# Other widths of the token pairs, another schedule for the weight factors, and another order of products in two groups

## The chip, the cores and the metric

The kernel runs on one core of a Trainium2 chip. The metric is device time in microseconds (us) of one execution; three runs of the kernel before give a median of 1737.24 us (1734.43 to 1738.43). The engines are TensorE (PE; its weight loads are listed apart as PEld), VectorE (DVE), ScalarE (ACT), GpSimd (POOL) and SyncE (SP), which issues all of this kernel's DMAs. Each engine takes its instructions in the order in which they were put to it.

## The reference

```python
def reference(q, k, v, moe_w_in, moe_w_out, moe2_w_in, moe2_w_out, moe2_alpha):
    # q, k, v: [8, 8, 576, 64]; attention inside chunks of 64 positions
    s = (q_c @ k_c.T) / sqrt(64);  a = softmax(s)
    x = (a @ v_c)                         # -> [4608 tokens, 512]
    h = x @ moe_w_in                      # 512 -> 2048
    x = (h * sigmoid(1.702 * h)) @ moe_w_out        # 2048 -> 512
    h = x @ moe2_w_in                     # 512 -> 2048
    g = max(h, 0) + alpha * min(h, 0)     # one alpha for each of 2048
    return g @ moe2_w_out                 # [4608, 512]
```

The weights arrive as 64-bit floats, taken as pairs of 32-bit words.

## The kernel before

A 64-bit weight is decoded on the chip: ACT takes the absolute value of the high word (L149), DVE puts a 32-bit float together in four passes (L152 to L167). For the matmuls each operand is split into a rounded part and the rest, and each product is made in three passes (high by high, low by high, high by low).

**First layer.** Nine blocks of 512 tokens, each with 16 slots, one for each 128 of the 2048 hidden features: 144 slots. In a slot `emit_h` (L446) runs 12 matmuls into `psH`, ACT's sigmoid (L460), DVE's product `g` (L462), ACT's rounding `gs` (L117) and the rest on DVE (L120). `emit_y` (L469) runs the 12 matmuls into `psY` of two slots earlier. Between these stand, by a table of half slots (`between`), the parts of the attention for later groups of 128 tokens: their loads (`load_qk`, `load_v`), transposes on DVE (L392), matmuls into `psS` and `psX`, the copies of `psX` on ACT (L417). A group of 128 tokens takes four slots. Where it crosses from one of the 8 batches to the next, its loads are cut in two.

**Preparation for the second layer.** The second layer's matrices are taken in halves and multiplied by a scheme of seven products for eight. Its seven weight factors of a block are made during the first layer in 32 steps, one every 3.25 slots from slot 18 on: `prep_load` reads a raw block of four quarters, `prep_abs` and `prep_decode` decode it, `prep_store_a` stores the three factors that are quarters themselves and lets POOL form four sums, `prep_store_b` stores the four others. Both split their four quarters (L222 on ACT, L223 on POOL) into the one tile `st2`, and write from it to DRAM. A loop at the end of the kernel puts the five parts of a step into slots n + 1, n + 2, n + 3, n + 4 and n + 6; each runs at the end of its slot. DMAs of the first layer wait in SP's order: a store that waits for its factors holds the raw loads and the attention's loads behind it.

**Second layer.** Tokens are taken in five pairs of two halves, of `PAIRS` columns each. A pair has four groups of 512 hidden features; a group has seven H products of 24 matmuls (two feature blocks `jj` of 12), in `H_ORDER`, and seven Y products of 24, in `Y_ORDER`. The H products use two accumulators, `psHa` for products 1, 6, 7 and 4, `psHb` for 2, 5 and 3; `ya` and `yb` likewise for Y. Products accumulate over one another (`start` at 1, 2 and 5 only), with read-outs between by ACT (L689, L663) and DVE (L692). The Y products of a group run between the H products of the next, so the first group's H products and the last group's Y products have no partner. `plan_group` gives each part of the work between H and Y a due time on a counter of products: the differences (L716), the rounding `o` on ACT (L706) and the rest on DVE (L711). DVE applies alpha at L666, and L775 and L777 add the Y results into `yacc`. `wi2t` (a ring of 9 tiles) and `w` (a ring of 4) hold the weights, loaded by SP one product at a time as tiles come free. A finished pair is written by `y_out` (L784) in 32 DMAs, the last one by `y_last`.

Of the kernel before, what the change touches and what calls it, by code (L numbers as in the profile page):

```python
# [9 lines left out]
F32 = mybir.dt.float32  # L10
F32R = mybir.dt.float32r
# [19 lines left out]
PREP_FROM = 18  # L31
PREP_EVERY = 3.25

PAIRS = (480, 480, 448, 448, 448)

H_ORDER = (1, 2, 6, 5, 7, 3, 4)
Y_ORDER = (1, 5, 6, 3, 7, 2, 4)
PLACE = {1: 0, 2: 1, 3: 6, 4: 2, 5: 3, 6: 4, 7: 5}

# [6 lines left out]
def tile_chunk_attention_two_ffn(  # L46
# [18 lines left out]
    P = 128  # L65
# [3 lines left out]
    GPB = NB // P  # L69
# [132 lines left out]
    def prep_store(step, lo, hi, t):  # L202
        kind, j, m = step
        dst = wi2[j][:, lo:hi, m] if kind == "wi" else wo2[j // 2][:, lo:hi, j % 2, m]
        nc.sync.dma_start(
            out=dst.rearrange("p i a f -> p i (a f)"),
            in_=t.bitcast(F32).rearrange("p i a f -> p i (a f)"),
        )
# [8 lines left out]
        except StopIteration as done:  # L217
            pr[step] = done.value[0].rearrange("p (q f) -> p q f", q=4)

    def prep_split(step, src):  # L220
        t = prep_p.tile([P, 4, 2, P], F32R, tag="st2", name="st2")
        nc.scalar.copy(t[:, :, 0], src)  # L222
        nc.gpsimd.tensor_tensor(out=t[:, :, 1], in0=src, in1=t[:, :, 0].bitcast(F32), op=ALU.subtract)  # L223
        return t

    def prep_store_a(step):
        u = pr[step]
        t = prep_split(step, u)
        prep_store(step, 0, 3, t[:, 0:3])
        sums = dec_p.tile([P, 4, P], F32, tag="u", name="sums")  # L230
        a11, a12, a22, a21 = (u[:, q] for q in range(4))
        for o, x, y, op in (
            (0, a21, a22, ALU.add), (1, sums[:, 0], a11, ALU.subtract),
            (2, a11, a21, ALU.subtract), (3, a12, sums[:, 1], ALU.subtract),
        ):
            nc.gpsimd.tensor_tensor(out=sums[:, o], in0=x, in1=y, op=op)
        pr[step] = sums

    def prep_store_b(step):
        t = prep_split(step, pr.pop(step))  # L240
        prep_store(step, 3, 7, t)


    def spans(t0, n):
# [17 lines left out]
    def load_qkv(g, names="qkv"):  # L262

        for nm in names:
            if g < GPB:
                t = {
                    "q": lambda: spare(f"wi{NF - GPB + g}", 0),
                    "k": lambda: spare(f"wi{NF - GPB + g}", 1),
                    "v": lambda: spare(f"wo{NF - 1 - g // 2}", g % 2),
                }[nm]()  # L270
            else:
                t = qkv_p.tile([P, 512], F32, tag=nm, name=nm, bufs=2)
            t = t.rearrange("p (h d) -> p h d", h=H)
            for off, n, b, s in spans(g * P, P):
                nc.sync.dma_start(
                    out=t[off:off + n],
                    in_={"q": q, "k": k, "v": v}[nm][b, :, s:s + n, :].rearrange("h p d -> p h d"),
                )
            qkv[g, nm] = t
# [289 lines left out]

    hs = [(p, gr, i, jj) for p in range(NP) for gr in range(NGR) for i in H_ORDER for jj in range(2)]
    ys = [(p, gr, i) for p in range(NP) for gr in range(NGR) for i in Y_ORDER]
    wi_order, wo_order, wi_q, wo_q = list(hs), list(ys), [], []
    turn = {"wi": 0, "wo": 0}
# [19 lines left out]
    def second_layer():  # L595
# [125 lines left out]
        def plan_group(p, gr, u):  # L721

            n = PAIRS[p]
            last = (p, gr) == (NP - 1, NGR - 1)
            times = (23, 25, 27, 30, 35, 39, 43) if last else (27, 30, 34, 36, 44, 46, 49)
            for i, nm, hi in zip(
                (1, 5, 6, 3, 7, 2, 4), ("g11", "t", "t", "g22", "t3", "g21", "t"), times
            ):
                at(u + hi, op_hi, p, gr, i, nm)
                at(u + hi + 1, op_lo, p, gr, i, nm)  # L730
            eng = nc.vector if last else nc.gpsimd
            t1, t2, t3, t4 = (24, 26, 29, 30) if last else (24, 32, 29, 38)
            at(u + t1, diff, n, "t", "g12", "g11", eng)
            at(u + t2, diff, n, "t", "g22", "t", eng)
            at(u + t3, diff, n, "t3", "g22", "g12", eng)
            at(u + t4, diff, n, "t", "g21", "t", nc.gpsimd)
# [122 lines left out]
    with tc.manual_schedule():  # L859
# [49 lines left out]
        ]  # L909
        for i, step in enumerate(steps):  # L910
            n = PREP_FROM + int(i * PREP_EVERY)
            for lag, fn in enumerate((None, prep_load, prep_abs, prep_decode, prep_store_a, None, prep_store_b)):
                if fn:
                    todo.setdefault(("prep", n + lag), []).append(partial(fn, step))


        between = {}
        for g in range(GPB, NG):
            for at, fn in zip((-4, -1, -1, 2, 5), (att_T, att_S, att_E, att_AT, att_PV)):
                if g > GPB or at > 0:  # L920
                    between.setdefault(8 * (g - GPB) + at, []).append((fn, g))
            if g + 1 < NG:
                between[8 * (g - GPB) + 5].append((load_v, g + 1))
            if g + 2 < NG:
                for part in range(8):
                    between.setdefault(max(0, 8 * (g - GPB) - 1 + part), []).append(
                        (partial(load_qk, part), g + 2)
                    )
# [4 lines left out]
        for n in range(NBLK * NF):  # L933
            blk, f = divmod(n, NF)
            for key in list(dec_t):
                split_w(*key)

            def middle():
                nonlocal dec
                for fn, g in between.get(2 * n, []):  # L940
                    fn(g)
                ahead = decode_w(todo.get(("decode", n + 1), []))
                next(ahead)
                for _ in dec:
                    pass
                dec = ahead

            emit_h(n, middle, nc.gpsimd if ("decode", n) in todo else nc.vector)


            ahead_y = {0: (n - 1,), 1: (), NF - 1: (n - 2, n - 1)}.get(f, (n - 2,))
            for m in ahead_y:
                if m >= 0:
                    emit_y(m)
            for fn, g in between.get(2 * n + 1, []):
                fn(g)
            for key in todo.get(("load", n), []):
                load_w(*key)
            for fn in todo.get(("prep", n), []):
                fn()  # L960
            if n == NBLK * NF - NF + 2:

                first.close()
                sec_p = ctx.enter_context(tc.tile_pool(name="second", bufs=1, reuse_waits="tile"))
                second_homes()
                x_load(0)
                for fn in x_sums(0):
                    fn()
            if n >= NBLK * NF - 12 and n % 2 == 0:
                i = H_ORDER[(n - (NBLK * NF - 12)) // 2] if n < NBLK * NF - 0 else None  # L970
                x_hi(0, i)
                x_lo(0, i)
            if n == NBLK * NF - 3:
                more_homes()
# [35 lines left out]
```

## Time and profile before

| what | us |
|---|---|
| median of three runs | 1737.24 |
| the profiled execution | 1733.37 |
| its span, first to last instruction | 1731.6 |
| PE busy | 1631.3 (94%) |
| weight loads on PE | 1366.9 (79%) |
| DVE busy | 1267.8 (73%) |
| ACT busy | 785.2 (45%) |
| POOL busy | 500.4 (29%) |

The profiled execution is one run under the hardware profiler. "Busy" sums the instructions of an engine; the matmuls are pipelined and weight loads overlap them, so a busy PE may still run below its best pace, which is read from the distance between the starts of equal groups of matmuls. The first layer ends near 997 us and the second begins there. The granted clock is 0.98 as a mean over the span.

### The profile page before, as it was taken

The page shows a single profiled execution, that of the slowest core. Times are in us where ns is not written, and L with a number is a line of the kernel's source. Part 1 is how long each engine was busy: PE and PEld are TensorE (multiplying, and loading weights), DVE is VectorE, ACT ScalarE, POOL GpSimd, SP SyncE. Part 2 cuts the span into 40 slices and gives each one's busy share as a digit, 9 for nine tenths or more (in the row PEclk, how much of TensorE's full clock was granted, in tenths as well). Part 3 has the DMA queues.
Part 4 walks back from the last instruction along what each step waited for, and adds up shares of the span by engine and source line. Part 5 has one row for each costly group of instructions (what it writes and reads, how often), then busy time and mean ns, then how long its engine had stood idle before and what let it go on. Part 6 is the DMA issues. An engine that isn't in the chain of part 4 may idle for free.

```text
span 1731.6 us, 25761 instructions
## 1 busy us (share of the span) xinstructions
PE 1631.3 (94%) x9257; PEld 1366.9 (79%) x9259; DVE 1267.8 (73%) x1858; ACT 785.2 (45%) x1098; POOL 500.4 (29%) x382
## 2 busy tenths in 40 slices
PE   7879998999988999989999989999999999999997
PEld 5667876777767777767788878888888998998996
DVE  7998666686666777757774347887788788788776
ACT  5554434344334443434433344555455455554542
POOL 3664122222212222212222024223422423422320
PEclk9999999999999999999999999999999999999999
DMA  8741334444334344334423067669667877977854
GB/s 229 215 115 36 73 88 110 114 109 111 93 92 107 107 110 115 101 97 118 100 62 125 0 214 249 203 180 293 214 204 194 309 217 193 313 212 192 278 180 121
DMA packets 388591, 268.11 MB, mean 155 GB/s; under 512 B 265840, under 2 KB 328048, under 8 KB 388464
## 3 DMA queue, kind: packets, MB, share of 16 engines
q1 hardware_dynamic: 388464, 266.47, 53.8%
q8 instruction: 73, 1.20, 0.3%
q14 instruction: 54, 0.44, 0.1%
HBM read 218.11 MB, written 48.23 MB: 154 GB/s over the span
## 4 chain that ended last, share of the span: by engine, by line
PE 45%; DVE 19%; DMA 8%; SPq 8%; ACT 7%; issue 4%; POOL 2%; DVEq 0%; ACTq 0%; POOLq 0%
PE psYa L759 10%; PE psHa L647 9%; PE psYb L759 7%; PE psHb L647 6%; SPq L297 6%; PE psH L453 6%; PE psY L476 5%; DMA raw<-in_moe_w_in_dram 3%; DMA raw<-in_moe_w_out_dram 3%; DVE g L462 2%; DVE g L666 2%; DVE at L392 2%; ACT gs L117 2%; DVE gs L120 1%; DVE o L711 1%
## 5 line engine op out<-in xcount | busy, mean ns | idle before, releaser
L453 PE MATMUL psH<-xs,wi 128*128 128x512 f32 x1728 | 442.7, 407 | 33.1 <-DVE g L462 29.5
L453 PEld LDWEIGHTS psH<-xs,wi 128*128 128x128 f32 x1728 | 330.6, 195 | 113.6 <-DVE g L462 37.8
L476 PE MATMUL psY<-gs,wo 128*128 128x512 f32 x1728 | 415.1, 390 | 3.6 <-ACT gs L117 3.6
L476 PEld LDWEIGHTS psY<-gs,wo 128*128 128x128 f32 x1728 | 323.7, 188 | 73.2 <-ACT gs L117 5.5
L117 ACT CAST gs<-g 128x512 fp32r<-128x512 f32 x144 | 89.3, 620 | 351.6 <-DVE g L462 351.6
L759 PE MATMUL psYa<-o,w 128*128 128x448 f32 (+1 forms) x960 | 218.6, 376 | 6.3 <-ACT o L706 3.8
L647 PE MATMUL psHa<-xop,wi2t 128*128 128x448 f32 (+1 forms) x960 | 216.0, 374 | 4.8 <-ACT g L663 4.4
L759 PEld LDWEIGHTS psYa<-o,w 128*128 128x128 f32 x960 | 180.2, 189 | 32.1 <-ACT o L706 5.1
L647 PEld LDWEIGHTS psHa<-xop,wi2t 128*128 128x128 f32 x960 | 181.7, 189 | 26.6 <-ACT g L663 4.8
L462 DVE TENSOR_TENSOR g<-psH,g 128x512 f32<-128x512 f32 x144 | 98.4, 683 | 138.5 <-ACT g L460 137.7
L666 DVE SCALAR_TENSOR_TENSOR g<-neg,minus_alpha,g 128x448 f32<-128x448 f32 (+1 forms) x160 | 182.7, 1182 | 6.8 <-ACT g L663 6.7
L759 PE MATMUL psYb<-o,w 128*128 128x448 f32 (+1 forms) x720 | 161.9, 373 | 0.0
L647 PE MATMUL psHb<-xop,wi2t 128*128 128x448 f32 (+1 forms) x720 | 160.1, 371 | 0.0
L120 DVE TENSOR_TENSOR gs<-g,gs 128x512 fp32r<-128x512 f32 x129 | 93.7, 726 | 88.6 <-ACT gs L117 87.9
L716 POOL TENSOR_TENSOR tsum<-g,tsum 128x896 f32<-128x896 f32 (+1 forms) x39 | 92.6, 2375 | 199.7 <-DVE o L711 196.9
L759 PEld LDWEIGHTS psYb<-o,w 128*128 128x128 f32 x720 | 134.8, 188 | 16.9 <-DVE o L711 0.6
L647 PEld LDWEIGHTS psHb<-xop,wi2t 128*128 128x128 f32 x720 | 135.2, 188 | 15.4
L716 POOL TENSOR_TENSOR tsum<-g,g 128x896 f32<-128x896 f32 (+1 forms) x19 | 41.6, 2188 | 350.9 <-DVE g L666 301.9
L392 DVE STREAM_TRANSPOSE at<-e 32x128 f32<-32x128 f32 x448 | 135.5, 302 | 6.7
L662 ACT ACTIVATE neg<-g 128x896 f32<-128x896 f32 (+1 forms) x60 | 58.5, 975 | 124.1 <-DVE g L692 124.1
L460 ACT ACTIVATE g<-psH 128x512 f32<-128x512 f32 x144 | 85.8, 596 | 50.7 <-PE psH L453 50.3
L711 DVE TENSOR_TENSOR o<-tsum,o 128x896 fp32r<-128x896 f32 (+1 forms) x60 | 66.5, 1109 | 46.1 <-ACT o L706 44.0
(117 smaller groups left out, 1898.8 us busy)
## 6 DMA issues: line engine op xcount, KB each, us to landing
wi2t<-wi SPq DMA_DIRECT2D x280, 256.0 KB, 3.8
w<-wo SPq DMA_DIRECT2D x140, 512.0 KB, 3.6
x<-ysb SPq DMA_DIRECT2D x36, 256.0 KB, 2.5
raw<-in_moe_w_in_dram SPq DMA_DIRECT2D x16, 512.0 KB, 5.4
raw<-in_moe_w_out_dram SPq DMA_DIRECT2D x16, 512.0 KB, 4.3
raw<-in_moe_w_in_dram SPq DMA_DIRECT2D x32, 256.0 KB, 3.9
wi<-st SPq DMA_DIRECT2D x16, 512.0 KB, 2.9
raw<-in_moe_w_out_dram SPq DMA_DIRECT2D x32, 256.0 KB, 3.5
```

What stands on the lines that cost most here:

```text
L117: nc.scalar.copy(hi, src)
L120: eng_lo.tensor_tensor(out=lo, in0=src, in1=hi.bitcast(F32), op=ALU.subtract)
L297: nc.sync.dma_start(out=t[r:r + SQ, h // 2, off // SQ:(off + n) // SQ], in_=src[b, h, s:s + n, y * SQ:(y + 1) * SQ].rearrange("(b t) e -> ...
L392: nc.vector.transpose(t[o * SQ:(o + 1) * SQ, :, i * SQ:(i + 1) * SQ], blocks[i * SQ:(i + 1) * SQ, :, o // 2, o % 2, :],)
L453: nc.tensor.matmul(ps, w[:, a, c], xs[:, b, c], start=(i == 0), stop=(i == 3 * KT - 1))
L460: nc.scalar.activation(out=g, in_=ps, func=AF.Sigmoid, scale=1.702)
L462: nc.vector.tensor_tensor(out=g, in0=ps, in1=g, op=ALU.mult)
L476: nc.tensor.matmul(y_t[j][t], w[:, a, t * P:(t + 1) * P], gs[:, b], start=(f == 0 and a + b == 0), stop=(f == NF - 1 and b == 1),)
L647: nc.tensor.matmul(ps, w[:, c, a], x[b][:, c], start=(k == 0 and i in (1, 2, 5)), stop=(k == 5 and i in (2, 3, 4)), skip_group_check=True,)
L666: nc.vector.scalar_tensor_tensor(out=g, in0=neg, scalar=minus_alpha[:, f:f + 1], in1=g, op0=ALU.mult, op1=ALU.add)
L716: eng.tensor_tensor(out=wide(homes[out], n), in0=wide(homes[x], n), in1=wide(homes[y], n), op=ALU.subtract,)
L759: nc.tensor.matmul(ps[:, d, :n], w[:, jj, d, a], x[b][:, jj], start=(k == 0 and i in (1, 5, 2)), stop=(k == 5 and i in (3, 2, 4)), skip_gr ...
```

## The change

The five pairs are 512, 512, 512, 384 and 384 columns wide in place of 480, 480, 448, 448 and 448; both add up to 2304. The first group of the second layer takes its H products in the order 1, 2, 6, 5, 7, 4, 3 (3 and 4 exchanged), the last group in the order 1, 2, 5, 6, 3, 7, 4, and the due times of the work of the first and of the last two groups are others. In the preparation the factors go through two tiles, `sta` with three factors and `stb` with four; the split for the first store handles three quarters in place of four; the absolute value runs in slot n + 3 right behind `emit_h`, where it stood at the end of slot n + 2; the second store comes in slot n + 5 in place of n + 6. `v` has one buffer in place of two from group 4 on, and its load is issued one slot later.

```diff
-PAIRS = (480, 480, 448, 448, 448)
+PAIRS = (512, 512, 512, 384, 384)
 H_ORDER = (1, 2, 6, 5, 7, 3, 4)
+H_FIRST = (1, 2, 6, 5, 7, 4, 3)
+H_LAST = (1, 2, 5, 6, 3, 7, 4)
...
-    def prep_split(step, src):
-        t = prep_p.tile([P, 4, 2, P], F32R, tag="st2", name="st2")
+    def prep_split(src, n, tag):
+        t = prep_p.tile([P, n, 2, P], F32R, tag=tag, name=tag)
         nc.scalar.copy(t[:, :, 0], src)
         nc.gpsimd.tensor_tensor(out=t[:, :, 1], in0=src, in1=t[:, :, 0].bitcast(F32), op=ALU.subtract)
         return t
 
     def prep_store_a(step):
         u = pr[step]
-        t = prep_split(step, u)
-        prep_store(step, 0, 3, t[:, 0:3])
+        prep_store(step, 0, 3, prep_split(u[:, 0:3], 3, "sta"))
...
     def prep_store_b(step):
-        t = prep_split(step, pr.pop(step))
-        prep_store(step, 3, 7, t)
+        prep_store(step, 3, 7, prep_split(pr.pop(step), 4, "stb"))
...
-                t = qkv_p.tile([P, 512], F32, tag=nm, name=nm, bufs=2)
+                t = qkv_p.tile([P, 512], F32, tag=nm, name=nm, bufs=1 if nm == "v" else 2)
...
+    FIRST_G, LAST_G = (0, 0), (NP - 1, NGR - 1)
+    h_order = {FIRST_G: H_FIRST, LAST_G: H_LAST}
...
-            times = (23, 25, 27, 30, 35, 39, 43) if last else (27, 30, 34, 36, 44, 46, 49)
+            times = {
+                FIRST_G: (27, 31, 36, 37, 44, 46, 49), LAST_G: (23, 22, 26, 28, 34, 38, 42),
+                (NP - 1, NGR - 2): (27, 30, 34, 33, 44, 46, 40),
+            }.get((p, gr), (27, 30, 34, 36, 44, 46, 49))
...
-            t1, t2, t3, t4 = (24, 26, 29, 30) if last else (24, 32, 29, 38)
+            t1, t2, t3, t4 = {FIRST_G: (28, 34, 30, 38), LAST_G: (20, 24, 28, 29)}.get(
+                (p, gr), (24, 32, 29, 38)
+            )
...
-            for lag, fn in enumerate((None, prep_load, prep_abs, prep_decode, prep_store_a, None, prep_store_b)):
-                if fn:
-                    todo.setdefault(("prep", n + lag), []).append(partial(fn, step))
+            for what, lag, fn in (
+                ("prep", 1, prep_load), ("abs", 3, prep_abs), ("prep", 3, prep_decode),
+                ("prep", 4, prep_store_a), ("prep", 5, prep_store_b),
+            ):
+                todo.setdefault((what, n + lag), []).append(partial(fn, step))
...
-                between[8 * (g - GPB) + 5].append((load_v, g + 1))
+                between.setdefault(8 * (g - GPB) + 7, []).append((load_v, g + 1))
...
             emit_h(n, middle, nc.gpsimd if ("decode", n) in todo else nc.vector)
+            for fn in todo.get(("abs", n), []):
+                fn()
```

On ACT, one step of the preparation in the first layer. Before (`u<-raw` is the absolute value, `st<-sums` and `st<-u` the splits for the second and the first store, `g` and `gs` the sigmoid and the rounding of a slot):

```order
L117 CAST gs<-g 128x512
L222 CAST st_5476<-sums 128x4x128
L149 ACTIVATE u<-raw_5434 128x512
L460 ACTIVATE g<-psH 128x512
L117 CAST gs<-g 128x512
L460 ACTIVATE g<-psH 128x512
L117 CAST gs<-g 128x512
L417 COPY x<-psX 128x4x64 x2
L222 CAST st_5608<-u 128x4x128
```

And now, the same place in the program:

```order
L225 CAST stb<-sums 128x4x128
L461 ACT_TABLE_LOAD
L461 ACTIVATE g<-psH 128x512
L120 CAST gs<-g 128x512
L461 ACTIVATE g<-psH 128x512
L120 CAST gs<-g 128x512
L152 ACTIVATE u<-raw_5438 128x512
L461 ACTIVATE g<-psH 128x512
L120 CAST gs<-g 128x512
L418 COPY x<-psX 128x4x64 x2
L225 CAST sta<-u 128x3x128
```

The absolute value has moved behind sigmoid and rounding of a later slot, and the two splits go to tiles of their own, the first of them with three quarters.

On PE, the first group of the second layer and the first Y matmuls, before:

```order
L647 MATMUL psHa<-xop,wi2t 128x480 x12
L647 MATMUL psHb<-xop,wi2t 128x480 x12
L647 MATMUL psHa<-xop,wi2t 128x480 x12
L647 MATMUL psHb<-xop,wi2t 128x480 x12
L647 MATMUL psHa<-xop,wi2t 128x480 x12
L647 MATMUL psHb<-xop,wi2t 128x480 x12
L647 MATMUL psHa<-xop,wi2t 128x480 x24
L647 MATMUL psHb<-xop,wi2t 128x480 x12
L759 MATMUL psYa<-o_9641,w_9625 128x480
```

And now:

```order
L653 MATMUL psHa<-xop,wi2t 128x512 x12
L653 MATMUL psHb<-xop,wi2t 128x512 x12
L653 MATMUL psHa<-xop,wi2t 128x512 x12
L653 MATMUL psHb<-xop,wi2t 128x512 x12
L653 MATMUL psHa<-xop,wi2t 128x512 x24
L653 MATMUL psHb<-xop,wi2t 128x512 x12
L653 MATMUL psHa<-xop,wi2t 128x512 x12
L653 MATMUL psHb<-xop,wi2t 128x512 x12
L770 MATMUL psYa<-o_9639,w_9623 128x512
```

The run of two products on `psHa` stood for product 4 and the next group's product 1; now it stands for products 7 and 4, with product 3 on `psHb` behind it.

On DVE, the last group's work ahead of its own first Y products, before (the four `g` with running numbers are g11, g12, g22 and g21 in that order):

```order
L777 TENSOR_TENSOR yacc<-psYa,yacc 128x2x448
L711 TENSOR_TENSOR o_9642<-tsum,o_9641 128x896
L666 SCALAR_TENSOR_TENSOR g_9634<-neg,minus_alpha,g_9634 128x448 x2
L711 TENSOR_TENSOR o_9644<-g_9633,o_9643 128x896
L716 TENSOR_TENSOR tsum<-g_9634,g_9633 128x896
L777 TENSOR_TENSOR yacc<-psYb,yacc 128x2x448
L711 TENSOR_TENSOR o_9646<-tsum,o_9645 128x896
L716 TENSOR_TENSOR tsum<-g_9635,tsum 128x896
L666 SCALAR_TENSOR_TENSOR g_9636<-neg,minus_alpha,g_9636 128x448 x2
L777 TENSOR_TENSOR yacc<-psYa,yacc 128x448 x2
```

And now:

```order
L672 SCALAR_TENSOR_TENSOR g_9632<-neg,minus_alpha,g_9632 128x384 x2
L698 TENSOR_TENSOR g_9633<-psHa,g_9633 128x768
L722 TENSOR_TENSOR tsum<-g_9632,g_9631 128x768
L788 TENSOR_TENSOR yacc<-psYa,yacc 128x2x384
L717 TENSOR_TENSOR o_9640<-tsum,o_9639 128x768
L672 SCALAR_TENSOR_TENSOR g_9633<-neg,minus_alpha,g_9633 128x384 x2
L717 TENSOR_TENSOR o_9646<-g_9631,o_9645 128x768
L722 TENSOR_TENSOR tsum<-g_9633,tsum 128x768
L788 TENSOR_TENSOR yacc<-psYb,yacc 128x2x384
L672 SCALAR_TENSOR_TENSOR g_9634<-neg,minus_alpha,g_9634 128x384 x2
L788 TENSOR_TENSOR yacc<-psYa,yacc 128x384 x2
```

Between the last two additions into `yacc` stand now the two steps of alpha for g21 alone; an `o` and a difference have moved ahead.

## Rows read from the trace of the kernel before

**Rows 1.** Busy time by stretch: window, us, engines, PE clock, DMA share, GB/s.

```profile
150.00:900.00 750.00, 699.71 (x4523) 559.76 (x4522) 523.14 (x1057) 305.04 (x495) 184.50 (x225) 0.98 0.39 100
1316.00:1700.00 384.00, 380.46 (x1850) 346.37 (x1848) 310.65 (x311) 198.04 (x229) 116.97 (x52) 1.00 0.77 232
```

**Rows 2.** Waits, 150 to 900 us: engine, releaser, total us, times, longest us.

```profile
ACT u L149 <- DMA raw<-in_moe_w_in_dram: 41.5, 13, 6.0
ACT u L149 <- DMA raw<-in_moe_w_out_dram: 41.1, 14, 5.0
...
PE psH L453 <- DVE g L462: 18.6, 8, 3.6
...
PE psS L340 <- ACT x L417: 13.6, 9, 3.6
PE psX L409 <- DVE at L392: 13.5, 17, 2.2
...
ACT st L222 <- DMA wi<-st: 9.1, 4, 6.1
ACT st L222 <- DMA wo<-st: 7.1, 2, 6.5
...
PE psY L476 <- ACT gs L117: 3.6, 3, 2.6
```

**Rows 3.** Timeline near 500 and 524 us: start, us, instruction, idle time before it.

```profile
499.09 1.21 SPq L199 DMA_DIRECT2D raw<-in_moe_w_in_dram  x2
...
504.07 0.66 ACT L149 ACTIVATE u<-raw 128x512 f32<-128x512 f32 x1 [5.97 <-DMA raw<-in_moe_w_in_dram]
...
506.92 1.98 PE L340 MATMUL psS<-kT,qT 64*64 64x64 f32 x32 [3.63 <-ACT x L417]
...
523.91 2.45 PE L453 MATMUL psH<-xs,wi 128*128 128x512 f32 x5 [3.24 <-DVE g L462]
```

**Rows 4.** ACT's groups, 150 to 900 us: busy us, mean ns, idle before.

```profile
L117 ACT CAST gs<-g 128x512 fp32r<-128x512 f32 x114 | 70.7, 620 | 304.1 <-DVE g L462 304.1
L460 ACT ACTIVATE g<-psH 128x512 f32<-128x512 f32 x113 | 67.3, 596 | 4.3 <-PE psH L453 3.9
```

**Rows 5.** PE's timeline at the starts of equal groups of matmuls.

```profile
989.41 8.32 PE L476 MATMUL psY<-gs,wo 128*128 128x512 f32 x36
997.57 2.76 PE L647 MATMUL psHa<-xop,wi2t 128*128 128x480 f32 x12
...
1207.27 2.76 PE L647 MATMUL psHa<-xop,wi2t 128*128 128x480 f32 x12
...
1280.38 2.58 PE L647 MATMUL psHa<-xop,wi2t 128*128 128x448 f32 x12
...
1351.40 2.60 PE L647 MATMUL psHa<-xop,wi2t 128*128 128x448 f32 x12
...
1420.21 2.64 PE L647 MATMUL psHa<-xop,wi2t 128*128 128x448 f32 x12
```

**Rows 6.** Timeline of two weight loads behind a wait.

```profile
1322.01 0.30 PEld L759 LDWEIGHTS psYa<-o,w 128*128 128x128 f32 x2 [0.80 <-DVE o L711]
```

**Rows 7.** PE's timeline at the end of the first group's products.

```profile
1021.05 5.01 PE L647 MATMUL psHa<-xop,wi2t 128*128 128x480 f32 x12 [4.43 <-ACT g L663]
```

**Rows 8.** Timelines of PE and DVE at the last group's first Y products.

```profile
1695.67 2.64 PE L759 MATMUL psYa<-o,w 128*128 128x448 f32 x12
...
1700.90 1.15 DVE L777 TENSOR_TENSOR yacc<-psYa,yacc 128x448 f32<-128x448 f32 x2
...
1702.15 3.99 PE L759 MATMUL psYa<-o,w 128*128 128x448 f32 x12 [3.84 <-ACT o L706]
```

**Rows 9.** SP's queue at a pair's start, first and last group of stores.

```profile
1310.74 4.12 SPq L794 DMA_DIRECT2D out_dram<-x_b  x8
...
1330.40 4.49 SPq L794 DMA_DIRECT2D out_dram<-x_t  x8
```

More of the change, by code (lines that the diff above doesn't have):

```diff
@@ L568, in x_lo @@
         )
-    hs = [(p, gr, i, jj) for p in range(NP) for gr in range(NGR) for i in H_ORDER for jj in range(2)]
+    FIRST_G, LAST_G = (0, 0), (NP - 1, NGR - 1)
+    h_order = {FIRST_G: H_FIRST, LAST_G: H_LAST}
+    hs = [
+        (p, gr, i, jj) for p in range(NP) for gr in range(NGR)
+        for i in h_order.get((p, gr), H_ORDER) for jj in range(2)
+    ]
     ys = [(p, gr, i) for p in range(NP) for gr in range(NGR) for i in Y_ORDER]
@@ L723, in plan_group @@
             n = PAIRS[p]
-            last = (p, gr) == (NP - 1, NGR - 1)
-            times = (23, 25, 27, 30, 35, 39, 43) if last else (27, 30, 34, 36, 44, 46, 49)
+            last = (p, gr) == LAST_G
+            times = {
+                FIRST_G: (27, 31, 36, 37, 44, 46, 49), LAST_G: (23, 22, 26, 28, 34, 38, 42),
+                (NP - 1, NGR - 2): (27, 30, 34, 33, 44, 46, 40),
+            }.get((p, gr), (27, 30, 34, 36, 44, 46, 49))
             for i, nm, hi in zip(
```

## The prediction

> **What bounds the kernel now.** I read four views in this order: the busy times by stretch, the table of waits, the timeline around the longest waits, and the SP queue's timeline. TensorE (PE) is the bound in both layers, and in different ways. From 150 to 900 us, where the first layer runs beside the attention and the preparation of the second layer's weights, PE is busy for 699.7 of 750 us; from 1316 to 1700 us, in the second layer, for 380.5 of 384 [rows 1]. So the first layer has about 50 us of holes to give back, and the second is paced by the matmuls themselves, with holes only at its start and its end.
>
> The waits of the first stretch [rows 2] say who makes the holes: PE waits 18.6 us for VectorE's (DVE's) product `g`, 13.6 us for ScalarE's (ACT's) copies of `psX`, 13.5 us for transposes on DVE, 3.6 us for ACT's `gs`, 49.3 us together. Behind ACT stand two causes of its own: 41.5 + 41.1 us, 27 times, in which its Abs (L149) waits for a raw weight block to land, and 9.1 + 7.1 us, 6 times, in which its cast into `st` (L222) waits for the last store out of the same buffer. ACT takes its instructions in order, so the next sigmoid stands behind both. One case [rows 3]: SP issues the raw load at 499.09, ACT reaches the Abs at 498.1 and stands 5.97 us; the copies of `psX` come after it, and PE stands 3.63 us for them.
>
> **The change, part by part.**
>
> *Preparation of the weights (32 steps).* In ACT's order the Abs moves from the end of slot n+2 to a place behind sigmoid and `gs` of slot n+3, one slot later, and the load stays where it was in its slot. In the first stretch a slot is 6.6 us on average (750 us for 114 casts of `gs`, one a slot [rows 4]). Even when ACT is late and runs sigmoid, `g` and `gs` without a gap, the Abs comes some 2 us later than now (sigmoid and `gs` 0.6 us each [rows 4], and between them DVE's product, which I take to be as long). Measured against a mean wait of 82.6/27 = 3.1 us and a longest of 6.0, most waits shrink to nothing and the longest to about 4. What is left falls behind `gs`, not ahead of the sigmoid. The cast waits go altogether: each of the two new tiles is reused after a whole step of 3.25 slots, 21 us, beside which the longest of these waits, 6.5 us, is short. The cast and subtraction of the first three factors handle 3 blocks and not 4. Added are a wait of DVE's decode for an Abs that now stands just before it, and one of the second cast, now a single slot behind the first, for GpSimd's (POOL's) sums; both chains (one Abs; a subtraction and four sums, at POOL's mean of 184.5/225 = 0.8 us [rows 1] some 4 us) are under a slot. `v` loses its second buffer, and its load waits for the last product with the old one; it is issued one slot later, behind that product, and is used three slots on. Behind it on SP stand q/k loads for two groups ahead, so I cost that at nothing; if SP stood a whole slot there, the next raw load would be late by it.
>
> What PE gets: of 13.6 + 3.6 us behind ACT I take 12; of 18.6 us behind `g` the two stalls that follow a cast wait (one at 523.91, 3.24 us) and smaller ones, 9; of 13.5 us for transposes, which come late where DVE waited for a sigmoid, 5. That is 26. SP is behind by several us where a group of 128 tokens crosses two batches and needs twice the loads, and those waits stay in part; for these and the added waits I give back 6: **-20 us**. Bounds: all 49.3 us gone on one side; on the other a loss, if the added waits cost more than the old ones (a rival below).
>
> *Widths.* The sum of columns is the same, 2304. From start to start twelve matmuls take (997.57 - 989.41)/3 = 2.72 us at 512 columns, (1280.38 - 1207.27)/28 = 2.611 at 480, (1420.21 - 1351.40)/28 = 2.4575 at 448 [rows 5], so 226.7, 217.6 and 204.8 ns for one. 384 is not in the trace. In proportion to 512 it would be 170 ns, by the line through 512 and 448 183; I take 177, the middle. For 512 in the second layer I take 227.5 (up to 231, if the 4 ns by which 480 and 448 lie above a line from 512 at the full clock's 0.417 ns a column belong to this layer). Before: 1344 x 217.6 + 2016 x 204.8 = 705.3 us. After: 2016 x 227.5 + 1344 x 177 = 696.5 us: **-9 us**, bounds 2016 x 226.7 + 1344 x 170 = 685.5 (-20) and 2016 x 231 + 1344 x 183 = 711.6 (+6).
>
> A weight load's record lasts 346.4/1848 = 187 ns, longer than 177, and weight loads are on record for 346.4 of 384 us [rows 1]. Two loads right behind a wait take 0.30 us together [rows 6]: the second starts some 110 ns after the first, so records overlap and 187 is no floor. The Trainium skill ("Perfetto Trace Analysis", Identifying the Most-Contended Engine) judges TensorE by the share of time in LDWEIGHTS; by it these stretches stand at 90% and 384 columns would need 187/177, over 100%. If that share binds, a matmul of 384 columns takes about 190 ns: a rival. The skill's "TensorE: Matmul & The Clock Gate" (LDWEIGHTS) gives columns/1.2, 107 ns for 128; the 0.30 us of [rows 6] agree with that, and by it nothing binds.
>
> *First group.* Its seven products run on PE without work of the second matmul between them. The eighth, the next group's first, waits 4.43 us for ACT's Relu from `psHa`, and PE then runs 12 matmuls at the lower clock level, 5.01 us for 2.76 [rows 5, 7]: 6.7 us lost. With product 4 ahead of 3, ACT has its Relus done while PE runs 3. But 7 and 4 now follow each other on bank a, and 4 waits for DVE's addition, like the 1.15 us of [rows 8] and the way there: 1.5 us. The Relus of 3 and the additions behind them reach the first `o` about 1.7 us after PE wants it. **-3.5 us** (bounds 0 and -6.7).
>
> *Last group.* PE stands 3.84 us at 1702.15 and loses 3.99 - 2.64 = 1.35 to the clock. The row names ACT's `o`, which had ended; what ended last is DVE's `yacc<-psYa`, done at 1702.05 [rows 8]: the bank is not read out. In the new order one `o` and one difference, about as long each as the read-out's 1.15, no longer stand between the two `yacc`, and the DVE work ahead is earlier. About 1.7 us remain (the read-out itself takes 1.15): **-3.5 us** (0 to -4). The end's transposes, additions and copies are a seventh narrower: **-1 us**.
>
> *Loads at the start of a pair.* Storing the finished pair puts four times 8 DMAs, 32 in all, of 4.12, 5.16, 5.65 and 4.49 us, 19.4 together, on SP (the first and the last of the four: [rows 9]); in these 24 us SP issues 3 + 4 weight loads, where five turns of two products (4.92 us each) use up 5 + 10. The four `w` tiles cover 4 x 4.92 = 19.7 us, less 5 to 7 us, by my estimate, from a tile's release to the landing of its next load. At 512 the turn is 5.4 us and the cover grows by as much as the stores. At 384 it is 4.25 us: 2.7 us less cover, and five turns leave SP 3 us less to catch up, with larger stores ahead of the first such pair: about 6 us short there and 2 at the next: **+8 us**, bounds 0 and 19.4 a pair, 39.
>
> Sum: -20 - 9 - 3.5 - 3.5 - 1 + 8 = **-29 us**. The profiled execution took 1733.4 us (span 1731.6); 1704.4 then, and the median of the runs lies 3.9 us above it: **1708 us**.
>
> **Rivals.**
> 1. *DVE or SP sets the first layer's pace*, and the ACT waits that go are replaced: PE gets 6 of 20 us back. For it: 11 of the 49 us are plain DVE work at block starts and transposes, and SP is full where groups cross. Against it: DVE is busy 523 of 750 us [rows 1]. 1722 us.
> 2. *Weight loads bind at 384*: 1344 x (190 - 177) = 17 us, less 6 since the ring then holds: 1719 us. For it the 187 ns; against it the overlap.
> 3. *The ring runs dry for longer*: another 12 us at two starts, with the clock falling in the gaps: 1720 us. For it that 448 columns is already near; against it that the loads catch up in one group.
> 4. *Slower: the raw block still lands late*, and the decode now stands right behind the Abs, so that ACT and DVE wait together and the next `g` behind them. If half of the 82.6 us reaches PE, 41 us in place of the 17 it pays now, the term of -20 becomes +24: 1752 us. It decides from +9 us in this term on (the others sum to -9). Against it: load and Abs are a slot further apart, and 3.1 us is under a slot.
>
> **Chances.** Forecast 0.55, with its own range 1695 to 1716; rival 1: 0.18; rival 2: 0.09; rival 3: 0.11; rival 4: 0.07. 1692 to 1730 leaves out rival 4 and the best corner. A difference under 0.2%, 3.5 us, can't be told from none. Faster than that 0.88, within 0.04, slower 0.08.
>
> **What would show it.** The waits of ACT's Abs from 82.6 us to under 35, its cast waits to none, and PE's waits from 150 to 900 us from 49 to about 30. Product starts 2.73 us apart at 512, 2.1 at 384 (2.28: rival 2). In the first group two short waits in place of one; at the last group's start under 2 us. Short waits for `w` or `wi2t` in the first twenty us of the two narrow pairs and nowhere else. Wrong it would be if the Abs waits stay, or if the wide and narrow pairs together take over 706 us.

## The result and the profile after

The changed kernel takes 1685.42 us (median of four runs, 1682.19 to 1689.17) beside 1737.84 before; the ratio is 0.9702, with a 95% interval of 0.9674 to 0.9730. The forecast was 1708 with a range from 1692 to 1730: the direction was right, and the size was 52 us where 29 were forecast, outside the range. One correction to the description above: a product of the second layer is 12 matmuls, two blocks of six, not 24; the prediction counts them as 12.

Where the time went is seen first at one point of the timeline, the start of the second layer. It was at 997.57 us [rows 5]; in the changed kernel it is at 951.42:

```profile
951.42 2.91 PE L653 MATMUL psHa<-xop,wi2t 128*128 128x512 f32 x12
...
966.64 3.03 PE L653 MATMUL psHa<-xop,wi2t 128*128 128x512 f32 x12 [1.39 <-DVE g L698]
...
979.05 2.81 PE L770 MATMUL psYa<-o,w 128*128 128x512 f32 x11 [0.96 <-DVE o L717]
982.36 3.04 PE L653 MATMUL psHa<-xop,wi2t 128*128 128x512 f32 x12 [0.50 <-ACT g L695]
...
1167.58 2.90 PE L653 MATMUL psHa<-xop,wi2t 128*128 128x512 f32 x12
...
1244.11 2.88 PE L653 MATMUL psHa<-xop,wi2t 128*128 128x512 f32 x12
...
1468.30 2.24 PE L653 MATMUL psHa<-xop,wi2t 128*128 128x384 f32 x12
...
1527.51 2.24 PE L653 MATMUL psHa<-xop,wi2t 128*128 128x384 f32 x12
```

So the first layer gave 46.1 us. From there to the end of the span it was 734.0 us before (1731.6 - 997.6) and is 729.0 now (1680.4 - 951.4): 5.0 us, in one profile of each kernel; the experiments below put the second layer's gain nearer to 2.5. Lines 966.64 to 982.36 are the first group, of which more below; the last four lines are the starts of equal pieces at either width, as in [rows 5].

The first layer's stretch of the changed kernel, cut so that it holds as many matmuls as [rows 1] did (the first of these two rows; the second is a stretch of the narrow pairs; columns as in [rows 1]):

```profile
150.00:855.00 705.00, 687.30 (x4525) 555.67 (x4524) 500.11 (x1056) 302.65 (x494) 170.48 (x224) 0.98 0.42 107
1468.00:1580.00 112.00, 110.22 (x621) 107.22 (x619) 92.71 (x105) 60.09 (x80) 37.13 (x19) 1.00 0.82 252
```

The same work takes 705 us in place of 750. Of these 45 us, 32.6 are idle time of PE (50.3 before, 17.7 now), and 12.4 come out of PE's busy time, 699.7 before. DVE is busy for 23 us less, 500.1 for 523.1. The waits of the same stretch, answering to [rows 2]:

```profile
DVE u L155 <- ACT u L152: 30.2, 6, 7.8
...
ACT stb L225 <- POOL sums L238: 13.5, 8, 1.9
ACT u L152 <- DMA raw<-in_moe_w_in_dram: 13.5, 5, 6.8
ACT u L152 <- DMA raw<-in_moe_w_out_dram: 12.0, 3, 7.8
...
PE psS L341 <- ACT x L418: 9.4, 4, 4.4
...
PE psX L410 <- DMA v<-in_v_dram: 5.8, 3, 2.3
...
PE psX L410 <- DVE at L393: 2.3, 7, 0.3
```

The Abs waits for raw blocks went from 82.6 us in 27 cases to 25.5 in 8 (one more, of 7.7 us, is put down to a load of `q`; before there were two, 5.6 us together). PE's waits for `g` (18.6 us) and for `gs` are gone, those for DVE's transposes went from 13.5 to 2.3. Both name DVE, whose instructions are the same as before.

### The profile page after: what moved, and what is told of

Same layout as the page of the kernel before. It is cut to its first block, busy times and chain, and to the rows that moved or that the text cites. A ratio compares the mean times of both kernels' runs of the same rounds, so it can differ in the third digit from the quotient of the medians.

```text
span 1680.4 us, 25742 instructions
## 1 busy us (share of the span) xinstructions
PE 1610.9 (96%) x9259; PEld 1342.0 (80%) x9259; DVE 1243.7 (74%) x1858; ACT 782.9 (47%) x1098; POOL 491.4 (29%) x382
## 4 chain that ended last, share of the span: by engine, by line
PE 61%; DVE 16%; SPq 4%; ACT 4%; DMA 3%; issue 3%; POOL 0%; DVEq 0%; ACTq 0%; POOLq 0%
PE psY L477 16%; PE psH L454 15%; PE psHa L653 8%; PE psYa L770 8%; PE psYb L770 6%; PE psHb L653 6%; SPq L298 3%; DVE g L672 3%; DVE o L717 2%; DVE yacc L788 2%; DVE at L393 2%; PE psS L341 2%; DVE g L698 1%; DVE xop L566 1%; DVE g L463 1%
## 5 line engine op out<-in xcount | busy, mean ns | idle before, releaser
L770 PE MATMUL psYa<-o,w 128*128 128x512 f32 (+1 forms) x960 | 216.2, 371 | 9.9 <-DVE o L717 3.6
L653 PE MATMUL psHa<-xop,wi2t 128*128 128x512 f32 (+1 forms) x960 | 211.8, 369 | 2.6 <-DVE g L698 1.9
L653 PEld LDWEIGHTS psHa<-xop,wi2t 128*128 128x128 f32 x960 | 175.1, 188 | 27.6 <-DVE g L698 2.7
L672 DVE SCALAR_TENSOR_TENSOR g<-neg,minus_alpha,g 128x512 f32<-128x512 f32 (+1 forms) x160 | 179.3, 1161 | 9.9 <-ACT g L669 9.7
L653 PE MATMUL psHb<-xop,wi2t 128*128 128x512 f32 (+1 forms) x720 | 158.8, 369 | 3.2 <-DMA wi2t<-wi 2.3
L770 PE MATMUL psYb<-o,w 128*128 128x512 f32 (+1 forms) x720 | 159.0, 368 | 0.1
L722 POOL TENSOR_TENSOR tsum<-g,tsum 128x1024 f32<-128x1024 f32 (+1 forms) x39 | 93.0, 2384 | 187.8 <-DVE o L717 187.8
L722 POOL TENSOR_TENSOR tsum<-g,g 128x1024 f32<-128x1024 f32 (+1 forms) x19 | 42.6, 2243 | 356.0 <-DVE g L672 220.2
L668 ACT ACTIVATE neg<-g 128x1024 f32<-128x1024 f32 (+1 forms) x60 | 58.6, 976 | 122.2 <-DVE g L698 122.2
L367 POOL TENSOR_TENSOR e<-e,d 128x512 f32<-128x512 f32 x32 | 33.5, 1046 | 253.9 <-DVE d L366 235.9
```

The lines of the kernel that those rows point to most:

```text
L653: nc.tensor.matmul(ps, w[:, c, a], x[b][:, c], start=(k == 0 and i in (1, 2, 5)), stop=(k == 5 and i in (2, 3, 4)), skip_group_check=True,)
L668: nc.scalar.activation(out=neg, in_=src, func=AF.Relu, scale=-1.0)
L672: nc.vector.scalar_tensor_tensor(out=g, in0=neg, scalar=minus_alpha[:, f:f + 1], in1=g, op0=ALU.mult, op1=ALU.add)
L722: eng.tensor_tensor(out=wide(homes[out], n), in0=wide(homes[x], n), in1=wide(homes[y], n), op=ALU.subtract,)
L770: nc.tensor.matmul(ps[:, d, :n], w[:, jj, d, a], x[b][:, jj], start=(k == 0 and i in (1, 5, 2)), stop=(k == 5 and i in (3, 2, 4)), skip_gr ...
```

## The experiments

Each ran beside the kernel before on one chip; they did not all run on the same one, so the ratios compare, and times only roughly. "Start" is where the second layer starts in its profile (997.6 before, 951.4 in the changed kernel).

| run | ratio to before (95%) | start, us |
|---|---|---|
| first layer's part alone | 0.9735 (0.9714 to 0.9755) | 956.4 |
| second layer's part alone | 0.9991 (0.9975 to 1.0007) | 997.5 |
| Abs moved alone | 0.9772 (0.9751 to 0.9793) | 959.4 |
| tiles, second store, v alone | 0.9889 (0.9864 to 0.9913) | 980.3 |
| raw loads earlier alone | 0.9806 (0.9782 to 0.9830) | 966.1 |
| second store sooner alone | 0.9942 (0.9925 to 0.9960) | 988.9 |
| changed, raw loads later | 1.0188 (1.0156 to 1.0220) | 1035.5 |
| changed, second store later | 0.9789 (0.9774 to 0.9804) | 965.9 |
| changed, one tile, two v | 0.9775 (0.9748 to 0.9802) | 957.1 |
| changed, load of v as before | 0.9727 (0.9705 to 0.9749) | 953.0 |
| changed, raw loads earlier | 0.9658 (0.9640 to 0.9676) | 940.4 |
| changed, orders as before | 0.9760 (0.9745 to 0.9775) | 953.1 |
| changed, narrow pair first | 0.9740 (0.9712 to 0.9768) | 952.9 |
| raw loads earlier, stores spread | 0.9663 (0.9646 to 0.9680) | 938.4 |

**The two halves of the change.** In the first run the widths, orders and due times are those of before, in the second the first layer is.

> The change's first-layer part alone (split tiles, place of Abs, second store, load of v); widths, orders and due times of the second layer as before. The trace of the changed kernel starts the second layer 46 us earlier and takes 5 us less in it. If both parts are independent: 1737.8 - 46 = 1692 us (1688 to 1696). If the widths gave the first layer something (the second layer's first loads overlap it), it stays above 1700.

> The second-layer part alone (widths, two orders, due times); the first layer as before. Independent parts: 1737.8 - 5 = 1733 us (1729 to 1736). My terms on record (-9 - 3.5 - 3.5 - 1 + 8 = -9) give 1729.

As far as the noise can tell they are independent: 1689.33 and 1732.56 us. Alone, the second layer's part can't be told from no change; from the first run to the changed kernel it is 0.33%, 5.7 us, with intervals that overlap. From the start of the second layer to the end of the span, the old second layer took 732.5 to 735.5 us in six profiles (734.1 in the mean), the changed one 729.0 to 734.0 in seven (731.6). So the gain is about 2.5 us, and the 5.0 us above are its best case.

**The Abs alone, and the rest of the first layer's part alone.**

```diff
-  prep_abs at the end of slot n + 2
+  prep_abs behind emit_h of slot n + 3       (first run of the two)
...
-  one tile st2, 4 quarters; store_b at n + 6; v: 2 buffers, load at half slot + 5
+  sta of 3, stb of 4; store_b at n + 5; v: 1 buffer, load at half slot + 7   (second)
```

> Before, with the Abs alone moved from the end of slot n+2 to behind sigmoid and gs of slot n+3. Theory A (the raw block's landing in ACT's order was the stall that mattered): at least 30 of the 46 us, 1708 us or less, with PE's idle time from 150 to 900 us near 25. Theory B (the one tile for the factors, its cast waits and the stores that wait on SP ahead of the raw loads, made most of it): 10 us at most, 1728 or more. Theory C (either alone is replaced by the other): both this and the next run gain under 15 us.

> Before, with the two tiles, three quarters in the first split, the second store a slot earlier, one buffer for v and its later load; the Abs stays at the end of slot n+2. Theory A: 1723 us or more (at most 15 gained). Theory B: 1708 or less. Theory C: over 1723, as the run above.

Theory A, at 1696.87: one line of the loop gives 39 of the 52 us. PE's waits with the Abs moved:

```profile
PE psH L456 <- DVE g L465: 16.4, 3, 6.7
ACT st L225 <- DMA wi<-st: 15.6, 4, 8.8
...
ACT st L225 <- DMA wo<-st: 9.9, 3, 8.6
ACT u L152 <- DMA raw<-in_moe_w_in_dram: 9.8, 5, 3.0
...
PE psX L412 <- DVE at L395: 5.0, 11, 0.7
ACT u L152 <- DMA raw<-in_moe_w_out_dram: 5.0, 2, 3.9
PE psS L343 <- ACT x L420: 4.2, 4, 1.9
PE psY L479 <- ACT gs L120: 0.7, 1, 0.7
```

The waits for transposes fell from 13.5 to 5.0 with not one DVE instruction changed. What is left behind `g` follows the cast waits, now 25.5 us (16.2 before). The second run took 1716.46, between the bounds of A and B: its Abs waits stayed at 80 us, and still it gained 19 us. That needed another cause. The two gains, 58 us together, are not a plain sum: the first layer's whole part gave 46.

**Time for the load, or place in ACT's order?** The load of the raw block is moved, and the Abs is not.

```diff
-  prep_load at the end of slot n + 1
+  n + 0 in the kernel before      (first run)
+  n + 2 in the changed kernel     (second run)
```

> Before, with the raw blocks' loads one slot earlier (end of slot n in place of n+1); the Abs stays at the end of slot n+2. Nothing on ACT moves. Theory A1 (what counts is the time between load and Abs): it gains like the move of the Abs alone, 25 to 40 us, 1698 to 1712, and ACT's Abs waits fall from 82.6 under 25 us. Theory A2 (what counts is that the Abs stands behind the sigmoid and gs, so that a late block holds up nothing that PE wants soon): under 12 us gained, 1724 or more.

> The changed kernel with the loads one slot later (end of slot n+2, the Abs behind gs in n+3), so that load and Abs stand less than a slot apart, as in the kernel before or closer. Theory A1: Abs waits of 70 us and more come back, and 20 us or more of time with them, 1705 or more. Theory A2: the waits come back behind gs, and the time stays within 8 us of the changed kernel's, 1694 at most.

A1, twice: 1702.12, and 1768.32, slower than before. In the first run no Abs waits for a raw block any more. In the second the Abs waits behind `gs`, 127.5 us in place of the 82.6 of the kernel before, and DVE's decode stands behind it:

```profile
DVE u L155 <- ACT u L152: 98.3, 22, 9.8
...
ACT u L152 <- DMA raw<-in_moe_w_in_dram: 70.1, 14, 9.8
ACT u L152 <- DMA raw<-in_moe_w_out_dram: 57.4, 15, 7.1
```

This is the mechanism of my rival 4. It is real, and the changed kernel's extra slot keeps clear of most of it. How much of the loss comes from the decode's place, and how much from longer waits, the run does not part.

**The second gain.** The second store is moved alone, out of the changed kernel and into the kernel before.

```diff
-  ("prep", 5, prep_store_b)
+  ("prep", 6, prep_store_b)     (first run; the second does the reverse in before)
```

> The changed kernel with the second store back at slot n+6; two tiles stay. Moving the Abs alone gained 39 us, the rest of the first-layer part alone 19, though Abs waits stayed there (80 us). Theory D: that second gain is DVE time. In the trace of before a decode pass (TENSOR_SCALAR, L152) takes 0.42 us alone and 1.55 us where POOL's subtraction (L223) runs beside it; the second store of a step at n+6 falls on the next step's decode, at n+5 it does not, and DVE's busy time over 114 slots goes from 523 to 500 us. Then this run has DVE at 515 us or more, passes of 1.5 us and more beside POOL, and is 8 to 17 us slower than the changed kernel: 1693 to 1702. Theory E: the gain came from the cast waits that the two tiles take away; then it stays within 4 us: 1689 at most.

> Before, with the second store alone a slot sooner (n+5); one tile, all four quarters, two v buffers, Abs as before. The second cast now follows the first store in the same tile by one slot, so cast waits grow beyond 16 us. Theory D: DVE falls under 508 us over 114 slots and the kernel gains 6 us or more: 1730 or less. Theory E: 1734 or more, or slower than before.

Theory D, both times: 1697.88 and 1725.80. In the first run the Abs waits for raw blocks stayed nearly as in the changed kernel (27.0 us for 25.5) and no cast waited for a store, but DVE was busy for 518.7 us in place of 500.1. The second run gives some 10 of the 19 us of the rest of the first layer's part (0.9942 beside 0.9889); there the Abs waits fell too, to 55.6 us, and the cast waits rose to 59.4. In the kernel before, POOL's subtraction and a DVE pass of the next step's decode, in the timeline:

```profile
309.49 1.31 POOL L223 TENSOR_TENSOR st<-sums,st 128x512 fp32r<-128x512 f32 x1 [6.40 <-ACT st L222]
309.53 1.55 DVE L152 TENSOR_SCALAR u<-u 128x512 f32<-128x512 f32 x1
311.12 0.43 DVE L157 TENSOR_SCALAR u<-u 128x512 int32<-128x512 int32 x1
```

A pass of 0.43 us takes 1.55: it ends 0.28 us after POOL's instruction. In this stretch 13 of the 33 passes of L152 took over 1 us, and each ended 0.28 us after an instruction of POOL. No table of waits shows it, because the profile counts it as busy; it shows in the means of one instruction's group. Two passes, of before first (150 to 900 us), then of the changed kernel (150 to 855):

```profile
L162 DVE SCALAR_TENSOR_TENSOR u<-raw,u 128x512 int32<-128x512 int32 x33 | 34.6, 1049 | 1.1
L152 DVE TENSOR_SCALAR u<-u 128x512 f32<-128x512 f32 x33 | 27.7, 840 | 0.0
```

```profile
L165 DVE SCALAR_TENSOR_TENSOR u<-raw,u 128x512 int32<-128x512 int32 x33 | 22.8, 692 | 1.1
L155 DVE TENSOR_SCALAR u<-u 128x512 f32<-128x512 f32 x33 | 14.3, 434 | 30.3 <-ACT u L152 30.2
```

That is 11.8 + 13.4 = 25 us of DVE, about as large as the fall of its busy time (23). With the second store of the changed kernel back at n + 6 the first of these passes has a mean of 1227 ns; the second keeps its 433, and the pass behind the first goes from 692 to 870. The Trainium skill ("SBUF — State Buffer", Who interferes with whom) says that VectorE and GpSimd share one pair of ports, and that when VectorE is in a mode with two ports, whichever of the two issues first has the pair for its whole instruction and the other is blocked. The trace agrees in what it shows, 1.55 us for 0.43; whether this pass ran in such a mode no run shows.

**What the two tiles are worth, and the load of v.**

```diff
-  sta and stb; v: 1 buffer, load at + 7
+  one tile st2; v: 2 buffers, load at + 5      (first run)
+  load of v at + 5                             (second run)
```

> The changed kernel with one tile of four quarters again and two v buffers with the load of v as before; Abs, second store's slot and the second layer as changed. The second cast now follows the first store in the same tile by a slot, and cast waits of 50 us and more come (59 in the run with the second store alone). If cast waits reach PE as Abs waits did (about half of them): 20 us or more slower than the changed kernel, 1705 or more. If they fall where ACT has time, because they stand behind gs: 1690 to 1697. If the tiles are worth nothing: 1688 or less.

> The changed kernel with the load of v back at the half slot of the last product that reads the one buffer. My prediction costs the move at nothing. If the load waits there on SP for PE, the raw loads and the q and k loads behind it are late: 3 to 15 us slower than the changed kernel. If not, within 3 us, and PE's 5.8 us of waiting for v go.

With one tile the cast waits come to 73.7 us, as the second cast stands a slot behind the first store, and the time is 1696.20, a ratio of 0.9775 beside 0.9702, with half widths of 0.0027 and 0.0028. It is the middle case: the waits cost something, far less than half of themselves. The sooner second store gains with one tile too (0.9942 above), and more with two. The place of v's load is worth nothing that these runs can tell (0.9727 beside 0.9702, intervals that overlap): PE's waits for `v` go, and those for `psX` copies grow from 9.4 to 16.4 us.

**What is left of the Abs waits.**

```diff
-  ("prep", 1, prep_load)
+  ("prep", 0, prep_load)
```

> The changed kernel with the loads one slot earlier as well (end of slot n, the Abs behind gs in n+3). The changed kernel's trace still has 33 us of Abs waits in 9 cases, and PE waits 9.4 us for psX copies behind them. If the time between load and Abs is all that counts, these go, and 4 to 10 us with them: 1675 to 1681. If what is left comes from SP, which is full where a group crosses two batches, or if the earlier load stands on SP for the one raw buffer: 1683 to 1695.

1675.51, better than either kernel. The Abs waits for raw blocks are down to 4.1 us, and the stretch of equal work is shorter again, with less idle time and less busy time of PE:

```profile
150.00:844.00 694.00, 679.62 (x4521) 550.99 (x4520) 499.39 (x1055) 302.11 (x492) 169.01 (x223) 0.99 0.41 109
```

**Orders, widths and stores of the second layer.** First the old orders and due times in the changed kernel, then a narrow pair at the start (384, 512, 512, 512, 384), then the kernel of the last experiment with half of each store three turns later:

```diff
-            for d in range(2):
-                for a in range(P // SQ): ... nc.sync.dma_start(...)
+            store(0)
+            at(now + 12, store, 1)
```

> The changed kernel with the old orders and due times in the second layer's first and last groups. My terms: 3.5 + 3.5 us lost, 1692. The two traces by stretches: the first group's waits and slow matmuls went from 7.5 to 3.8 us, the last two groups' from 5.4 to about 4: 1690. If the order matters less at these widths: 1687 or less.

> The changed kernel with pairs of 384, 512, 512, 512 and 384. Now only the last pair is narrow behind a pair's stores, so of the four waits for wi2t and w at the two narrow starts (5.8 us in the profile of the changed kernel) about half should go: 1682 to 1684 where the changed kernel runs 1685. If the first group at 384 loads faster than DMAs deliver, it loses as much or more at the start: 1686 to 1692.

> The changed kernel with the raw loads a slot earlier (1675.5 us in its run) and, of each of a finished pair's four groups of stores, the second half put three turns later on SP. The stores take the same time in sum. The profile of the run without this has 6.4 us of waits for wi2t and w at the two narrow starts. If the stores ahead of the loads make them: under 2.5 us of such waits and 1669 to 1673. If SP or the DMA engines are short over the whole stretch: as many waits, only later, and 1674 to 1678.

The orders: 1693.39, some 10 us slower than with the new ones (0.9760 for 0.9702); of these the profile of this run has 4 us more in waits for weights than the changed kernel's, which I can't put down to the orders. In its profile the stalls at the first and at the last group are back, 4.65 us (and 5.29 us for the twelve matmuls behind it) and 3.8. A narrow pair at the start brings a wait of 2.57 us for `wi2t` in the first group and keeps those of the last pair: 1690.42, a ratio whose interval overlaps the changed kernel's. The spread stores changed nothing that can be measured, 1675.99 for 1675.51; in one profile of each, the waits for `w` and `wi2t` moved within the first narrow pair and went at the second.

## Why the prediction was wrong, step by step

*The preparation, -20: wrong, -46.1.* This is the step that failed, in its paragraph "What PE gets". Over equal work PE's idle time fell by 32.6 us where the step had 26 less 6, and PE's busy time, which had no term, fell by 12.4; PE's waits in the table came to 17.5 us where about 30 were forecast. The step has three errors.

First, it shared out PE's waits by the engine that the table names, and took for DVE's own what was ACT's. The Abs wait delays a sigmoid, DVE stands for it, its transposes and its next `g` are late, and the table names DVE. I took 9 of 18.6 us and 5 of 13.5; moving the Abs alone took transposes from 13.5 to 5.0, and the whole change took `g` from 18.6 to nothing.

Second, it took 49.3 us of waits for all that could be had. PE's busy time was no floor: at equal counts of matmuls it fell from 699.7 to 687.3, and with the loads a slot earlier to 679.6, where the layer had gained 57.2 us (997.6 - 940.4). The products that feed on transposes show how: before, `psX<-at,v` had 27.5 us of busy time for 928 matmuls, now 23.1. Waits too short for the table stand inside busy time, as do matmuls at the lower clock behind a wait. In this stretch the granted clock was at its lower level, 1.2 GHz, for 30.7 us before, for 23.9 in the changed kernel and for 13.7 with the loads a slot earlier. At half the pace that is some 3 of the 12.4 us, and 8 to 9 of the 20.1 in the last of the three, by this estimate; the rest is not parted further.

Third, it counted the sooner second store as an added wait and nothing more. It gave 8.6 us alone (start 988.9), where it takes POOL off the next decode. The prediction read DVE's 523 busy us [rows 1] as work; some 25 of them were standing still.

The 6 us that this step gave back were right in their cause: the waits where a group crosses two batches did stay. Of the 17.5 us of PE's waits left in the table, 15.7 stand at three places (272 to 286, 501 to 512 and 726 to 737 us), each behind a run of 24 loads of `k` that holds SP for 11.8 to 12.9 us. There the raw load goes out after ACT has come to the Abs, at the second of them (from 498.45 on):

```profile
501.28 1.23 SPq L202 DMA_DIRECT2D raw<-in_moe_w_in_dram  x2
...
502.12 4.59 PE L454 MATMUL psH<-xs,wi 128*128 128x512 f32 x12
...
506.14 0.67 ACT L152 ACTIVATE u<-raw 128x512 f32<-128x512 f32 x1 [7.69 <-DMA q<-in_q_dram]
...
511.95 0.27 PE L341 MATMUL psS<-kT,qT 64*64 64x64 f32 x2 [2.49 <-ACT x L418]
```

What was too small was the gain everywhere else. Rival 1 is out by its time, 1722 us; the full SP that it named is what is left.

What held of this step: the Abs waits were forecast at under 35 us and came to 25.5, and the cast waits went. The extra slot is what did it, as said. Added waits came where named, DVE's decode for the Abs (30.2 us in 6 cases), the second cast for the sums (13.5), and PE for v (5.8), which I had costed at nothing.

*Widths, -9: right.* From 1167.58 to 1244.11 and from 1468.30 to 1527.51 there are 28 products each: 2.733 and 2.115 us, 227.8 ns for a matmul of 512 columns and 176.2 for one of 384 (guessed 227.5 and 177). 2016 x 227.8 + 1344 x 176.2 = 696.1 us for 705.3. Rival 2 is refuted by the second row of the windows above: weight loads are on record for 107.2 of 112 us in the narrow pairs, and a matmul takes 176.2 ns, not the 190 of that rival. A share of 96% in weight loads is not a bound here. This gain in pace is not yet time: with the old orders the new widths gained nothing that the runs show (0.9760, beside 0.9735 for the first layer's part alone).

*First group, -3.5: right.* 1.39, 0.96 and 0.50 us in place of 4.43 and 2.25 at the lower clock: -3.8. I had named the first two, at 1.5 and 1.7. That the order did it is shown by the run with the old orders, where the wait is back.

*Last group, -3.5: too much.* The changed kernel's timeline at its last two groups:

```profile
1627.90 1.31 PE L653 MATMUL psHb<-xop,wi2t 128*128 128x384 f32 x6 [0.88 <-DVE g L698]
...
1645.41 2.36 PE L653 MATMUL psHa<-xop,wi2t 128*128 128x384 f32 x12 [0.55 <-DVE g L698]
...
1652.41 1.14 DVE L672 SCALAR_TENSOR_TENSOR g<-neg,minus_alpha,g 128x384 f32<-128x384 f32 x2
1653.47 1.01 DVE L788 TENSOR_TENSOR yacc<-psYa,yacc 128x384 f32<-128x384 f32 x2
...
1654.58 1.65 PE L770 MATMUL psYa<-o,w 128*128 128x384 f32 x8 [2.63 <-issue]
```

PE's three waits are 4.1 us together, for 3.84 + 1.35 = 5.2: -1.1. At 384 columns PE comes to the bank sooner, and DVE's read-out still has alpha for g21 ahead of it. The -1 for the end did not come: from the last Y matmul to the end of the span it was 8.9 us and is 9.2.

*Loads at a pair's start, +8: near.* Two waits in each narrow pair and none elsewhere, as forecast, 5.2 us in sum:

```profile
1456.69 1.31 PE L653 MATMUL psHb<-xop,wi2t 128*128 128x384 f32 x6 [1.11 <-DMA wi2t<-wi]
1459.90 2.32 PE L770 MATMUL psYa<-o,w 128*128 128x384 f32 x12 [1.89 <-DMA w<-wo]
...
1580.61 1.33 PE L653 MATMUL psHb<-xop,wi2t 128*128 128x384 f32 x6 [1.19 <-DMA wi2t<-wi]
1582.94 2.34 PE L770 MATMUL psYa<-o,w 128*128 128x384 f32 x12 [1.00 <-DMA w<-wo]
```

In this profile the clock did not fall behind them. In each of the other six profiles of the same second layer, twelve matmuls behind a wait in the first narrow pair did run at the lower clock. With the raw loads later, they did so behind nearly the same waits, 1.16 and 1.85 us: from 1543.96 on, twelve matmuls took 4.18 us in place of 2.24. In the run of the second layer's part alone the four waits are 5.9 us and the slow matmuls behind them 3.4 more, 9.3 in all. Rival 3 wanted 20 and is out by its size, though the falling clock that it named is there. My cause, the stores ahead on SP, is open: spread stores took the second pair's waits away and made the first pair's longer.

The terms for the second layer add up to -9.2 - 3.8 - 1.1 + 0.3 + 5.2 = -8.6. This profile gave 5.0, and the means of the profiles give 2.5, not the 9 of the forecast. The falling clock behind the loads is a part of the difference; where the rest went stays open. Against -26 us in the first layer that is little.

## What to carry to other kernels

When engines take their work in order, a table of waits names the last link of a chain. Before a gain is shared out by engine, ask what the named engine was itself waiting for, and credit the whole chain to its head; and do not take the busy time of the bound engine for a floor. Compare the mean of each group with the same instruction undisturbed: a pass that stands still beside another engine is booked as work, and a step moved by one slot may take it out of the way.

## What the runs showed of the hardware that was not expected

A DVE pass beside a POOL subtraction took 1.55 us for 0.43, and 12 of the 33 such passes before took over 1.5; each of the 13 that took over 1 us ended 0.28 us after POOL's instruction. After nearly the same waits at a pair's start the granted clock stayed up in one profile (1.11 and 1.89 us) and fell in another (1.16 and 1.85), where twelve matmuls took 4.18 us for 2.24. Matmuls of 384 columns took 176.2 ns each while the records of weight loads lasted 107.22/619 = 173 ns, in 96% of the time.
